# Splitting the first expert's weight chunks at other steps of the last head pair, in an attention and mixture-of-experts kernel

## The chip, the cores and the metric

The kernel runs on one core of one Trainium2 chip. A core has five engines that work side by side, each through its own list of instructions in order: TensorE (PE; its weight loads, PEld, overlap the matmuls), VectorE (DVE), ScalarE (ACT), GpSimd (POOL) and SyncE (SP), which here only issues DMA transfers. Engines wait for one another through semaphores. The metric is the time of one execution on the device in microseconds; lower is better. Times come as medians of several runs, and one further execution is recorded by the hardware profiler.

## What is computed

Attention over 8 batches and 8 heads, with queries averaged in pairs, and then a mixture of 8 experts on its output, each token going to the one expert with the highest logit:

```python
    q_pool = q.reshape(B, H, S // factor, factor, D).mean(axis=3)
    scores = scale * np.matmul(q_pool, k.transpose(0, 1, 3, 2))
    scores = scores - np.max(scores, axis=-1, keepdims=True)
    attn = np.exp(scores)
    attn = attn / (np.sum(attn, axis=-1, keepdims=True) + 1e-09)
    return np.matmul(attn, v).astype(np.float32)
...
    logits = x @ w_gate + modality_bias[modality_id]
    e_idx = np.argmax(logits, axis=1)
...
    for e in range(E):
        mask = e_idx == e
        h = np.maximum(x[mask] @ w1[e], 0.0)
        out[mask] = gate_w[mask, None] * (h @ w2[e])
```

Sizes: sequence 1152 (576 pooled queries), head width 64, 4608 tokens of 512 values, w1 of 512 x 1024 and w2 of 1024 x 512 for each expert. Inputs are f32; the kernel keeps f32 accuracy by splitting operands into a high and a low 16-bit part and multiplying three times.

## The kernel before

**Attention.** Two batches are taken together, so there are 32 pairs of heads. Each pair takes 18 steps of a loop (`for t in range(NSTEP * npairs)` in `attention`), 576 in all. A step emits work in a fixed order of letters: maximum pass of a later pair (`maxpass`: matmuls on PE, line 837, and reductions on DVE, line 838), score matmuls (lines 904 and 905) with their exponentials on ACT (line 906), and value products (`pv`, lines 963 to 965). A value product takes three matmuls for 128 queries: the high part of the exponentials `Pe` with the high and the low values, and the low part `Pl` with the values. `Pl` is made from `Pe` by a *lowering* (line 887 on ACT, 889 on DVE). Four pairs of buffers `Pe`/`Pl`, numbered 0 to 3, go round; one holds three of the nine key chunks of a head. After the last value product of a head, `evac` (lines 981 to 986) divides by the sums, and `split_x` (lines 923 and 933) splits the output into high and low parts.

Other work is hung into the steps. A table of numbers says at which step, counted from the pair's first, each piece is emitted; `at(t, p, fn)` puts it at the end of step `t`, `later(n, fn)` n steps on. Beside this there is a list of side jobs written as Python generators: `yield n` means "go on n steps later". For each of the four groups of 9 token tiles, `route` computes from the logits the gate values and the expert of each token; after group 2, `first_list` makes the token lists of the first six blocks of the expert stage (blocks 0 to 5) from the first three groups. Its steps follow one after another from where `route` ends.

**The last pair** (steps 558 to 575) has no maximum pass beside it. There the first expert is prepared, in four pieces per weight matrix: `load_first` loads chunk q of w1 into a tile of the attention that is no longer used (`rawq`, two of `rawk`, `rawv`), at the steps in `T_W0`; `split_first` splits it at the steps in `T_W1`: the high part on ACT (line 1584, 128 x 1024) and, at the end of the same step, the low part on DVE (line 1586). `gather_first` and `turn_first` gather and transpose the tokens of block 0 (`xfirst`, lines 1208 to 1222).

**Experts.** Blocks of 256 tokens, one expert each, follow on PE without a pause: `gemm1` multiplies by w1 (lines 1312 to 1314, 96 matmuls), `gemm2` by w2 (lines 1411 to 1413). The next chunks come through five raw buffers: `load_w` on SP's queue (line 1280 for w1, 1283 for w2), `split_w` on ACT and DVE (lines 1295 and 1296); a load waits until the chunk that used its buffer is split. The tokens of block j are gathered by POOL (line 1198), split into `xs` (lines 1262, 1263) and turned by four DMA transposes on SP's queue into `xpart` (line 1268), a high and a low part for each half of 128 tokens; `gemm1` of the block needs all four. The expert stage's raw buffers and gather buffers lie where the attention's tiles lay, so the first loads and gathers wait for the last readers of those tiles, the splits of line 1586 among them.

The order on PE, ACT, DVE and POOL is the order of emission within a stage; where the attention ends and the experts begin, and for the transfers on SP, the recording layer interleaves instructions by its own estimate of when they can start. So moving a piece can also change what stands around it elsewhere.

Of the kernel before, what the change touches and what calls it, by code (L numbers as in the profile page):

```python
# [118 lines left out]
NF = 4  # L119
T_W0 = (1, 3, 2, 3)  # L120
W1D = 0
T_W1 = (6, 4, 10, 11)
E1 = 1
E2 = 0
COPY = (lambda nc: nc.vector.tensor_copy, lambda nc: nc.scalar.copy, lambda nc: nc.gpsimd.tensor_copy)
# [38 lines left out]
class Router:  # L164
# [113 lines left out]
    def route(self, g, eng):  # L278

        nc, sm, rs = self.nc, self.sm, RS[g]  # L280
        while self.added[g] < H // 2:
            yield 1
        big = [sm.tile([P, 3, NT, E], F32, name=f"wide{i}") for i in range(2)]
        lg = big[0][:, 0]
        nc.vector.tensor_reduce(lg, self.lg[g].rearrange("p t (w e) -> p t e w", w=3), op=ALU.add, axis=AX.X)
        ts = slice(g * NT, (g + 1) * NT)
        bc = lambda a: a.unsqueeze(2).broadcast_to([P, NT, E])
        be = lambda a: a.unsqueeze(1).broadcast_to([P, NT, E])
        w, w2 = big[0][:, 1], big[0][:, 2]
        inv = sm.tile([P, NT], F32, name="inv")  # L290
        nc.gpsimd.tensor_scalar(inv, self.mid[:, ts], -1.0, 1.0, op0=ALU.mult, op1=ALU.add)
        nc.gpsimd.tensor_tensor(w, be(self.b0[:, 0]), bc(inv), op=ALU.mult)
        nc.gpsimd.tensor_tensor(w2, be(self.b0[:, 1]), bc(self.mid[:, ts]), op=ALU.mult)
        nc.gpsimd.tensor_tensor(w, w, w2, op=ALU.add)
        yield rs
        nc.gpsimd.tensor_tensor(lg, lg, w, op=ALU.add)
        yield rs + 1
        mx = sm.tile([P, NT], F32, name="mx")
        nc.vector.tensor_reduce(mx, lg, op=ALU.max, axis=AX.X)
        nc.vector.tensor_tensor(lg, lg, bc(mx), op=ALU.subtract)  # L300
        yield rs
        nc.scalar.activation(w, lg, AF.Exp)
        key = big[1][:, 0]
        nc.vector.scalar_tensor_tensor(key, lg, 0.0, be(self.ieE), op0=ALU.is_ge, op1=ALU.mult)
        kmin = sm.tile([P, NT], F32, name="kmin")
        nc.vector.tensor_reduce(kmin, key, op=ALU.min, axis=AX.X)
        yield rs
        oh = sm.tile([P, NT, E], BF16, name="oh16")
        nc.vector.tensor_tensor(oh, key, bc(kmin), op=ALU.is_equal)
        yield 1  # L310
        nc.gpsimd.tensor_scalar(self.exp[:, ts], kmin, float(E), None, op0=ALU.add)
        yield rs
        sx = sm.tile([P, NT], F32, name="sx")
        nc.vector.tensor_reduce(sx, w, op=ALU.add, axis=AX.X)
        gt = sm.tile([P, NT, 2], F32, name="gt")
        ts2 = sm.tile([P, 2], F32, name="ts2")
        nc.vector.tensor_reduce(ts2[:, 0:1], self.scales[g].bitcast(F32), op=ALU.max, axis=AX.X)
        yield 1
        nc.gpsimd.tensor_scalar(sx, sx, EPS, None, op0=ALU.add)
        nc.gpsimd.tensor_scalar(ts2[:, 0:1], ts2[:, 0:1], 1.0 / XSC, None, op0=ALU.mult)  # L320
        yield 1
        nc.vector.reciprocal(ts2[:, 1:2], ts2[:, 0:1])
        nc.vector.reciprocal(gt[:, :, 0], sx)
        nc.vector.tensor_scalar(gt[:, :, 0], gt[:, :, 0], ts2[:, 0:1], 1.0 / WSC ** 2, op0=ALU.mult, op1=ALU.mult)
        nc.gpsimd.tensor_copy(gt[:, :, 1], ts2[:, 1:2].broadcast_to([P, NT]))
        eng.dma_start(out=self.xs[g * NT * P:(g + 1) * NT * P, DM:XW].rearrange("(t p) d -> p t d", p=P), in_=gt)
        yield rs
        for _ in range(self.lr - 1):
            yield
        pr = self.pm(4)[:, 0:(NT + 1) * E].rearrange("p (t e) -> p t e", e=E)  # L330
        nc.tensor.matmul(pr[:, 0:NT], self.up, oh, start=True, stop=False, skip_group_check=True)
        for s in range(NT):
            nc.tensor.matmul(pr[:, s + 1:], self.on, oh[:, s:s + 1].broadcast_to([P, NT - s, E]), start=False, stop=s == NT - 1,
                             skip_group_check=True)
        yield 1
        pos = big[1][:, 2]
        nc.vector.tensor_tensor(pos, pr[:, 0:NT], be(self.base), op=ALU.add)
        nb = self.keep.tile([P, E], F32, name="base")
        nc.vector.tensor_tensor(nb, pr[:, NT], self.base, op=ALU.add)
        self.base = nb  # L340
        yield rs
        nc.gpsimd.tensor_tensor(pos, pos, oh, op=ALU.mult)
        yield rs
        nc.vector.tensor_reduce(self.pos[:, ts], pos, op=ALU.add, axis=AX.X)
# [241 lines left out]
def attention(tc, ctx, att, ident, npairs, xpool, on_two, on_split, on_scale, jobs, side, set_pm, started, ahead, hip):  # L586
# [419 lines left out]
    def later_end(n, fn):  # L1006
        at_end.setdefault(now[0] + n, []).append(fn)

    def at(t, p, fn, end=True):
        if 0 <= p < npairs:  # L1010
            (at_end if end else todo).setdefault(max(t, 0), []).append(fn)
# [120 lines left out]
    if ahead:  # L1132
# [10 lines left out]
        for i in range(NF):  # L1143
            at(last + T_W0[i], 0, lambda i=i: ahead[2](i, room[i]))
            at(last + T_W1[i], 0, lambda i=i: later_end(W1D, ahead[3](i)))
    running, wait = [], 0
# [496 lines left out]
```

## Time and profile before

| | us |
|---|---|
| median of 3 runs (lowest, highest) | 1127.96 (1127.93, 1128.63) |
| the profiled execution, its own time | 1128.69 |
| span of its records | 1126.9 |
| granted TensorE clock, mean | 0.997 of full |
| DVE / ACT / POOL busy in the span | 86% / 81% / 37% |

The profile page gives for each engine the busy time in the span, and the trace answers further questions: busy time by stretch, instructions in order of time, and for each idle stretch of an engine the instruction that ended it (in brackets: idle us, and after the arrow the engine, the tile and the line that was waited for). A row of the timeline has the start in us, the duration, the engine, the line of the kernel, the operation, and output <- inputs; "x3" means that three in a row are merged. Matmuls are pipelined: one of 65 columns takes 0.19 us from start to end, but the next starts 0.03 us after it. `SPq` and `POOL DMA` rows are the issues of transfers, not the transfers themselves.

### The profile page before, as it was taken

To read this page: it belongs to the slowest core of one execution; us is meant where nothing else is said; L and a number is where in the kernel's file an instruction comes from. 1 tells how busy PE (TensorE), PEld (TensorE's weight loads), DVE (VectorE), ACT (ScalarE), POOL (GpSimd) and SP (SyncE) were. 2 spreads that over 40 slices of the span, in tenths; PEclk is the share of its full clock that TensorE was granted. 3 is DMA by queue.
4 is the path that set the end of the run, shared out by engine and by line. 5 is a ranking of instruction groups with operands and counts; after the bars stand their busy time and mean duration, and the time that the engine had idled before them with its cause. 6 is when DMAs were issued, how large, how long until landed. Compare 5 with 4: busy or idle time off the path is not lost. (4 is left out here: it accounts for less than half of the span.)

```text
span 1126.9 us, 36809 instructions
## 1 busy us (share of the span) xinstructions
PE 1102.1 (98%) x15053; PEld 812.6 (72%) x15053; DVE 972.7 (86%) x1971; ACT 914.8 (81%) x1469; POOL 413.9 (37%) x408
## 2 busy tenths in 40 slices
PE   7999999999999999999999999999999999999997
PEld 3777777777777777777777777777667667667674
DVE  7999999999999999999999999877997756756754
ACT  5999999999999999999999998876656656655654
POOL 7853344355434444443445333115213122121111
PEclk9999999999999999999999999999999999999999
DMA  7667757758769678678687563599999999999993
GB/s 230 181 184 171 194 161 188 186 156 190 172 164 208 155 179 181 165 179 190 163 185 170 160 149 94 147 310 282 281 265 269 309 284 275 277 280 281 270 267 107
DMA packets 175522, 232.67 MB, mean 206 GB/s; under 512 B 92303, under 2 KB 126751, under 8 KB 175344
## 3 DMA queue, kind: packets, MB, share of 16 engines
q1 hardware_dynamic: 169254, 210.45, 71.8%
q0 software_dynamic: 6080, 19.78, 6.5%
q8 instruction: 120, 1.97, 0.8%
q14 instruction: 58, 0.48, 0.1%
q10 hardware_dynamic: 10, 0.00, 0.0%
HBM read 146.11 MB, written 18.99 MB: 147 GB/s over the span
## 5 line engine op out<-in xcount | busy, mean ns | idle before, releaser
L906 ACT ACTIVATE Pe<-psc 128x432 int32<-128x432 f32 x768 | 376.9, 526 | 41.0 <-PE psc L905 32.4
L838 DVE TENSOR_REDUCE mp<-pm 128x1 f32<-128x512 f32 x566 | 371.6, 684 | 17.1 <-PE pm L837 10.4
L963 PE MATMUL xp<-VH,Pe 128*128 128x65 f16 x2880 | 372.5, 193 | 0.0
L965 PE MATMUL xp<-VS,Pl 128*128 128x65 f16 x2880 | 371.9, 193 | 0.4 <-DVE Pl L889 0.4
L964 PE MATMUL xp<-vl,Pe 128*128 128x64 f16 x2880 | 370.6, 192 | 0.0
L964 PEld LDWEIGHTS <-Pe 128*128 128x128 f16 x2880 | 267.6, 98 | 87.6
L905 PE MATMUL psc<-B 65*128 65x432 f16 (+2 forms) x1152 | 304.7, 287 | 1.0 <-DMA B<-mr 1.0
L904 PE MATMUL psc<-B 128*128 128x432 f16 (+2 forms) x1152 | 304.0, 286 | 1.7 <-ACT Pe L906 1.5
L963 PEld LDWEIGHTS <-Pe 128*128 128x128 f16 x2880 | 272.0, 98 | 42.7 <-issue 5.2
L965 PEld LDWEIGHTS <-Pl 128*128 128x128 f16 x2880 | 266.5, 97 | 0.6 <-DVE Pl L889 0.6
L887 ACT ACTIVATE Pl<-Pe 128x1152 f16<-128x1152 uint16 (+1 forms) x190 | 219.2, 1154 | 6.0
L837 PE MATMUL pm<-hi,QB 128*128 128x512 f16 x566 | 213.8, 379 | 4.1 <-DVE mp L838 3.0
L1314 PE MATMUL ph<-xpart,w1l 128*128 128x256 f16 x544 | 148.3, 273 | 0.0
L1312 PE MATMUL ph<-xpart,w1h 128*128 128x256 f16 x544 | 148.3, 273 | 0.0
L1313 PE MATMUL ph<-xpart,w1h 128*128 128x256 f16 x544 | 148.3, 273 | 0.0
L784 POOL TENSOR_SCALAR VH<-rawv,sc 128x512 f16<-128x512 f32 (+1 forms) x60 | 103.6, 1736 | 76.2 <-PE pm L837 35.6
L905 PEld LDWEIGHTS <-B 65*128 65x128 f16 x1152 | 112.8, 98 | 25.3 <-issue 2.5
L904 PEld LDWEIGHTS <-B 128*128 128x128 f16 x1152 | 112.5, 98 | 7.9 <-issue 2.5
L1318 DVE SCALAR_TENSOR_TENSOR hl<-ph,hh 128x512 f16<-128x512 f32 x72 | 49.7, 690 | 73.3 <-ACT hh L1317 47.8
L1317 ACT ACTIVATE hh<-ph 128x512 f16<-128x512 f32 x72 | 43.0, 598 | 84.8 <-PE ph L1314 81.6
L1412 PE MATMUL po<-w2l,hh 128*128 128x512 f16 x288 | 109.2, 379 | 0.0
L1413 PE MATMUL po<-w2h,hl 128*128 128x512 f16 x288 | 109.2, 379 | 0.0
(274 smaller groups left out, 1877.6 us busy)
## 6 DMA issues: line engine op xcount, KB each, us to landing
w2r<-in_w_dram SPq DMA_DIRECT2D x76, 512.0 KB
w1r<-in_w_dram SPq DMA_DIRECT2D x72, 512.0 KB
rawv<-in_att_dram SPq DMA_DIRECT2D x32, 576.0 KB
B<-hi SPq DMA_DIRECT2D x128, 144.0 KB
rawq<-in_att_dram SPq DMA_DIRECT2D x31, 576.0 KB
rawk<-in_att_dram SPq DMA_DIRECT2D x31, 576.0 KB
B<-qh SPq DMA_DIRECT2D x128, 72.0 KB
B<-lo SPq DMA_DIRECT2D x64, 144.0 KB
```

Source lines behind the costliest of these rows:

```text
L837: nc.tensor.matmul(pm, QB[p % 2][:, u], s["hi"][:, t * 512:(t + 1) * 512], start=True, stop=True)
L838: nc.vector.tensor_reduce(mp[:, u, t:t + 1], pm, op=ALU.max, axis=AX.X)
L887: nc.scalar.activation(low, rest, AF.Copy, scale=LOW)
L904: nc.tensor.matmul(o, b1[:, ks], b1[:, qs], start=True, stop=False, skip_group_check=True)
L905: nc.tensor.matmul(o, b2[:, ks], b2[:, qs], start=False, stop=True, skip_group_check=True)
L906: nc.scalar.activation(Pe[:, D + x0:D + x1], pt, AF.Exp, scale=1.0 / 16)
L963: nc.tensor.matmul(out, Ph[:, qs], vh[:, c, j, 0:D + 1], start=c == 0 and g == 0, stop=False, skip_group_check=True)
L964: nc.tensor.matmul(out[:, 0:D], Ph[:, qs], vl[:, c, j], start=False, stop=False, skip_group_check=True)
L965: nc.tensor.matmul(out, Pl[:, qs], vs[:, c, j, 0:D + 1], start=False, stop=c == NKC - 1, skip_group_check=True)
L1312: nc.tensor.matmul(o, hi[:, c, fs], xh[:, :, c], start=c == 0, stop=False)
L1313: nc.tensor.matmul(o, hi[:, c, fs], xl[:, :, c], start=False, stop=False)
L1314: nc.tensor.matmul(o, lo[:, c, fs], xh[:, :, c], start=False, stop=c == 3)
```

## The change

```diff
-T_W1 = (6, 4, 10, 11)
+T_W1 = (9, 6, 14, 16)
...
         nc.vector.reciprocal(ts2[:, 1:2], ts2[:, 0:1])
         nc.vector.reciprocal(gt[:, :, 0], sx)
+        if g == 2:
+            yield 1
         nc.vector.tensor_scalar(gt[:, :, 0], gt[:, :, 0], ts2[:, 0:1], 1.0 / WSC ** 2, op0=ALU.mult, op1=ALU.mult)
```

Chunk 0 is split at step 9 instead of 6 of the last pair, chunk 1 at 6 instead of 4, chunk 2 at 14 instead of 10, chunk 3 at 16 instead of 11. In `route` of the third group the multiplication of the gates, with the copy and the store behind it, goes one step later (step 475 instead of 474), and with it every later piece of `route` and `first_list` up to step 554, which is now 555. What is left of `first_list` at step 557 is emitted there at once, before and after. No instruction is added or removed. The two new lines move the numbers of all later lines by 2 in the changed kernel.

**The end of the last pair, on DVE.** `Pl_120` and `Pl_122` are the low parts of buffers 2 and 3, which hold the last six key chunks, `w1l` the low part of a weight chunk, `x_17728` the output of `evac`. Before:

```order
L889 TENSOR_SCALAR Pl_120<-Pe_119 128x864
L981 TENSOR_SCALAR rs<-xp 128x5
L982 RECIPROCAL rr<-rs 128x5
L986 SCALAR_TENSOR_TENSOR x_17728<-xp,sc,rr 128x5x64
L889 TENSOR_SCALAR Pl_120<-Pe_119 128x864
L1222 TENSOR_TENSOR xfirst<-pm,xfirst 128x256 x2
L889 TENSOR_SCALAR Pl_122<-Pe_121 128x864 x2
```

With the change:

```order
L891 TENSOR_SCALAR Pl_120<-Pe_119 128x864
L983 TENSOR_SCALAR rs<-xp 128x5
L984 RECIPROCAL rr<-rs 128x5
L988 SCALAR_TENSOR_TENSOR x_17728<-xp,sc,rr 128x5x64
L1588 SCALAR_TENSOR_TENSOR w1l_18284<-rawk,w1h_18283 128x1024
L891 TENSOR_SCALAR Pl_120<-Pe_119 128x864
L1224 TENSOR_TENSOR xfirst<-pm,xfirst 128x256 x2
L891 TENSOR_SCALAR Pl_122<-Pe_121 128x864
L1588 SCALAR_TENSOR_TENSOR w1l_18340<-rawv,w1h_18339 128x1024
L891 TENSOR_SCALAR Pl_122<-Pe_121 128x864
```

Chunks 2 and 3 now stand between the last lowerings; before they stood ahead of the first row shown.

**The same place on PE.** The last value products (`xp`) and the first matmuls of the first expert (`ph`). Before, all value products come first:

```order
L965 MATMUL xp<-VS_126,Pl_122 128x65
L1312 LDWEIGHTS w1h_18052
L1312 MATMUL ph<-xfirst,w1h_18052 128x256
L1313 LDWEIGHTS w1h_18052
L1313 MATMUL ph<-xfirst,w1h_18052 128x256
```

With the change seven matmuls of the expert stand ahead of the last 25 of the value products; these are the rows where they end:

```order
L1316 MATMUL ph<-xfirst,w1l_18147 128x256
L1314 LDWEIGHTS w1h_18146
L1314 MATMUL ph<-xfirst,w1h_18146 128x256
L967 LDWEIGHTS Pl_122
L967 MATMUL xp<-VS_126,Pl_122 128x65
L965 LDWEIGHTS Pe_121
L965 MATMUL xp<-VH_125,Pe_121 128x65
```

The seven stand right ahead of a matmul that needs the second half of `Pl_122`.

**The start of the experts, on SP.** `xpart_18595` is the turned input of block 1: `xs_18597` and `xs_18598` are the high and low part of its first half, `xs_18602` and `xs_18603` of its second; `w1r_18516` is the fourth chunk of w1 for block 1, `w2r_18518`, `18524`, `18559` and `18610` its chunks of w2, `w1r_18625` the first of block 2. Before:

```order
L1268 DMA_TRANSPOSE xpart_18595<-xs_18597 128x4x128
L1268 DMA_TRANSPOSE xpart_18595<-xs_18602 128x4x128
L1268 DMA_TRANSPOSE xpart_18595<-xs_18598 128x4x128
L1268 DMA_TRANSPOSE xpart_18595<-xs_18603 128x4x128
L1280 ISA
L1280 DMA w1r_18516<-in_w1_dram 128x1024
```

With the change (the middle is left out: the loads `w2r_18518`, `w2r_18524`, `w2r_18559`):

```order
L1270 DMA_TRANSPOSE xpart_18595<-xs_18597 128x4x128
L1270 DMA_TRANSPOSE xpart_18595<-xs_18598 128x4x128
L1282 ISA
L1282 DMA w1r_18516<-in_w1_dram 128x1024
...
L1285 DMA w2r_18610<-in_w2_dram 128x1024
L1282 ISA
L1282 DMA w1r_18625<-in_w1_dram 128x1024
L1270 DMA_TRANSPOSE xpart_18595<-xs_18602 128x4x128
L1270 DMA_TRANSPOSE xpart_18595<-xs_18603 128x4x128
```

The transposes of the second half have moved behind six loads.

## The prediction

> **What bounds the kernel now.** First the page's table of engines, then busy time by stretch, to see which engine sets the end in the stages that the change touches.
>
> ```profile
> PE 1102.1 (98%) x15053; PEld 812.6 (72%) x15053; DVE 972.7 (86%) x1971; ACT 914.8 (81%) x1469; POOL 413.9 (37%) x408
> 600.00:700.00 100.00, 96.22 (x1650) 74.04 (x1647) 96.85 (x242) 92.83 (x158) 41.14 (x34) 1.00 0.61 141
> 712.00:736.00 24.00, 22.57 (x485) 19.40 (x482) 19.37 (x45) 19.92 (x38) 5.17 (x4) 1.00 0.65 207
> 736.00:900.00 164.00, 164.00 (x1212) 113.07 (x1209) 134.22 (x235) 104.35 (x137) 42.76 (x42) 1.00 1.00 284
> 900.00:1100.00 200.00, 200.00 (x1386) 135.45 (x1385) 129.12 (x152) 118.36 (x152) 36.76 (x37) 1.00 0.99 275
> ```
>
> The columns of a stretch are its length and the busy time of PE, PEld, DVE, ACT and POOL, then the granted clock and the DMA share. PE is busy 98% of the span at full clock, and from 736 to 1100 us without a gap. So nothing but PE's own gaps can be won, and a gap made in the expert stage is added to the end in full, because no later gap absorbs it. The gaps that the change can reach lie in the last pair of heads, 712 to 736 us (24.00 - 22.57 = 1.43 us idle), and around the third group's gates, near 610 us. The chain that ended last tells little here: its lines hold 1% of the span together.
>
> The gaps of the last pair, in PE's timeline (start, duration, idle before and its releaser in brackets):
>
> ```profile
> 720.41 0.19 PE L965 MATMUL xp<-VS,Pl 128*128 128x65 f16 x1
> 721.17 0.28 PE L904 MATMUL psc<-B 128*128 128x288 f16 x1 [0.57 <-ACT Pe L906]
> 728.70 0.19 PE L964 MATMUL xp<-vl,Pe 128*128 128x64 f16 x1
> 728.73 0.19 PE L965 MATMUL xp<-VS,Pl 128*128 128x65 f16 x1
> 729.34 0.34 PE L904 MATMUL psc<-B 128*128 128x432 f16 x1 [0.42 <-ACT Pe L906]
> 730.27 0.19 PE L964 MATMUL xp<-vl,Pe 128*128 128x64 f16 x1
> 730.89 0.20 PE L965 MATMUL xp<-VS,Pl 128*128 128x65 f16 x1 [0.43 <-DVE Pl L889]
> ```
>
> In flow these matmuls start 0.03 us apart (728.70 and 728.73), so the real losses are 0.76, 0.61 and 0.62 us less 0.03 each: **1.90 us**, more than the idle column says. Their causes stand on ACT and DVE:
>
> ```profile
> 719.64 1.06 ACT L1584 ACTIVATE w1h<-rawk 128x1024 f16<-128x1024 f32 x1 [0.77 <-DMA rawk<-in_w_dram]
> 724.82 0.77 ACT L923 ACTIVATE x<-x,sc 128x576 f16<-128x576 f32 x1
> 725.90 1.06 ACT L1584 ACTIVATE w1h<-rawk 128x1024 f16<-128x1024 f32 x1
> 727.26 1.07 ACT L1584 ACTIVATE w1h<-rawv 128x1024 f16<-128x1024 f32 x1
> 726.99 1.22 DVE L1586 SCALAR_TENSOR_TENSOR w1l<-rawk,w1h 128x1024 f16<-128x1024 f32 x1
> 728.36 1.23 DVE L1586 SCALAR_TENSOR_TENSOR w1l<-rawv,w1h 128x1024 f16<-128x1024 f32 x1
> 726.14 0.38 DVE L275 TENSOR_TENSOR lg<-pm,lg 128x216 f32<-128x216 f32 x1
> 729.50 0.81 DVE L933 SCALAR_TENSOR_TENSOR x<-x,sc,x 128x576 f16<-128x576 f32 x1
> 730.75 0.75 DVE L1222 TENSOR_TENSOR xfirst<-pm,xfirst 128x256 f16<-128x256 f32 x2
> 732.35 0.55 DVE L986 SCALAR_TENSOR_TENSOR x<-xp,sc,rr 128x320 f32<-128x320 f32 x1
> 734.00 1.12 DVE L889 TENSOR_SCALAR Pl<-Pe 128x864 f16<-128x864 uint16 x2
> ```
>
> Chunk 1's ACT half waited 0.77 us for its load with the exponentials queued behind it, hence the gap at 721. Chunks 2 and 3 stand one exponential apart on ACT, and their DVE halves back to back, hence the gaps at 729 and 731.
>
> **The change, part by part.** Nothing is added or removed in work: four ACT operations of 1.06 us and four DVE operations of 1.2 us move later, and one DVE operation of the gates moves a step.
>
> *Splits.* Chunk 1 at step 6 comes after its load has landed and alone: 0.73 us is won. Chunk 0 at step 9 stands on ACT right behind the operation of line 923. That one starts at 724.82 now and, with PE 0.73 earlier, near 724.0; chunk 0's ACT half ends near 725.7. From there DVE has no gap until the last lowering. In the order of the changed kernel it does: low part of chunk 0 (1.2), logits (0.3), two lowerings of Pe1 with line 933 between (0.6 + 0.75 + 0.55), xfirst (0.65), lowering (0.5), evacuation (0.85), low part of chunk 2 (1.2), lowering (0.5), xfirst (0.65), lowering (0.5), low part of chunk 3 (1.2), lowering (0.55). That is 10.0 us by the rows above (each less about 0.08, by which neighbours overlap; a lowering is half of the row at 734.00, the evacuation is line 986 with two small ones ahead); it ends near 735.6. Now the same last lowering ends at 734.00 + 1.12 = 735.12. PE runs 1.9 us ahead of today up to its last score products, less about 0.2 before Pe1's lowering, and so is done with them near 731.9 (733.60 now: the row at 733.41 below, and 0.19 until the next). Then it meets three new waits, by the same running sum: Pe2's second lowering, behind chunk 2, is there at 732.65 and wanted two value products later, at 732.05; Pe3's first at 733.8, wanted at 733.4; Pe3's second, behind chunk 3, at 735.6, wanted at 734.4. The last is partly covered, because seven matmuls of the first expert now stand in front of it (96 of them take 736.0 to 746.6 in the row below, so 7 take about 0.76 us). After the last lowering PE has 25 matmuls left, 25 x 0.03 = 0.75 us: the attention ends at 736.3 with 0.76 us of the expert done, worth 735.55.
>
> ```profile
> 733.41 0.35 PE L905 MATMUL psc<-B 65*128 65x432 f16 x1
> L1312 PE MATMUL ph<-xfirst,w1h x32: 272/273/276, 736.0 to 746.6; 128*128 128x256 f16 x32
> ```
>
> Now the first expert starts at 736.0, so the gain is **0.45 us** of the 1.90. Bounds: 1.90 won if DVE catches up, 0.8 lost if DVE ends 0.5 late and the seven matmuls cover nothing. I take 0.45.
>
> *What the splits free.* The raw tiles hold buffers that the expert's loads and gather need:
>
> ```profile
> 728.25 3.03 SPq L1283 DMA_DIRECT2D w2r<-in_w_dram  x4
> 729.85 1.28 POOL L1198 DMA_INDIRECT xg<-xs,giA  x1 [12.24 <-DVE w1l L1586]
> 743.39 5.51 SPq L1268 DMA_TRANSPOSE xpart<-xs  x4
> 749.16 0.37 SPq L1280 DMA_DIRECT2D w1r<-in_w_dram  x1
> 753.65 1.06 ACT L1295 ACTIVATE w1h<-w1r 128x1024 f16<-128x1024 f32 x1 [2.90 <-DMA w1r<-in_w_dram]
> 755.99 1.76 SPq L1280 DMA_DIRECT2D w1r<-in_w_dram  x2
> 757.80 0.27 PE L1312 MATMUL ph<-xpart,w1h 128*128 128x256 f16 x1
> ```
>
> The first load starts at 728.25, when chunk 2's low part ends (726.99 + 1.22), the gather when chunk 3's does (728.36 + 1.23). With chunk 2's end near 732.1 and chunk 3's near 735.0 both come 4 to 5 us later. What covers this: w2's first chunk is needed by line 1411 only after the 96 matmuls of w1, which end at about 747, and the gathered rows by the transposes at 743.39. These covers hold; if they were gone, up to 5 us would show.
>
> The cost that I do count is on SP's queue. All four transposes of block 1 now stand together at 743.39, 5.51 / 4 = 1.38 us each. In the changed kernel the second half's two stand behind six more loads. The last of the six waits until the fourth w1 chunk of block 1 is split on DVE. That chunk's load, held until 749.16 now, goes right after two transposes, near 746.2; its ACT half no longer waits 2.90 us but stands behind its neighbour, done at 751.75; its DVE half at 753.1 (1.2 each). So the sixth load goes at 753.2 and the two transposes at 753.5 and 754.8. When does such data arrive?
>
> ```profile
> DMA packets 504, 0.18 MB, mean 368 GB/s; under 512 B 489, under 2 KB 489, under 8 KB 504
> DMA packets 48, 0.20 MB, mean 393 GB/s; under 512 B 0, under 2 KB 0, under 8 KB 48
> 757.96 1.19 SPq L1268 DMA_TRANSPOSE xpart<-xs  x1
> DMA packets 314, 0.18 MB, mean 360 GB/s; under 512 B 286, under 2 KB 286, under 8 KB 314
> ```
>
> These are the DMA packets of 750.0 to 750.5, of 757.0 to 757.5 (loads alone: no small packets) and of 761.0 to 761.5. Small packets mark the transposes. Block 1's fourth, issued from 747.5 (743.39 + 5.51 - 1.38), was still moving at 750.0 to 750.5, 3.0 us after its start; block 2's first, issued at 757.96 among loads, at 761.0 to 761.5, 3.0 to 3.5. So the last transpose, from 754.8, is there at 757.8 to 758.3. PE wants it at 757.80 - 0.45 - 0.1 = 757.25. Stall: **0.5 to 1.1 us, I take 0.6**; bounds 0 (if the fourth chunk goes earlier) and 3 (if the loads that start 5 us later push the whole chain by 1.5 us, and the transposes wait among loads for 1 us more).
>
> The Trainium skill, "DMA: Bandwidth & Descriptors", section "Anatomy of one DMA — SWDGE (gpsimd) path", speaks against the change here: a transfer's semaphore fires only when the last byte is confirmed written, about 2.0 us of fixed cost. No row here shows that lag by itself; by it the stall would be near 2.5 us, and the sum, as an estimate, 1.9 us slower; that outcome is a rival below.
>
> *Gates.* DVE is full in this stage (96.85 of 100 us).
>
> ```profile
> 609.70 0.23 DVE L324 TENSOR_SCALAR gt<-gt,ts 128x9 f32<-128x9 f32 x1
> 609.84 0.68 DVE L838 TENSOR_REDUCE mp<-pm 128x1 f32<-128x512 f32 x1
> 610.58 0.38 PE L845 MATMUL pm<-hi,QB 128*128 128x128 f16 x4 [0.90 <-DVE mp L838]
> 611.97 0.38 PE L837 MATMUL pm<-hi,QB 128*128 128x512 f16 x1 [0.46 <-DVE mp L838]
> ```
>
> PE waits 0.90 us for the reduction at 609.84. One operation ahead of it (609.84 - 609.70 = 0.14 us) moves behind the next two: the reduction ends 0.14 earlier, **0.15 us** won. The small write of the gates now stands behind three moves on SP; only the gathers after the token list read it. Everything of this group up to the token list slides one step too: the same operations, between other reductions, on a DVE that stays full. Bounds for gates and slide together: 1.4 won (0.90 and the 0.46 behind it) and 0.7 lost. I take 0.15.
>
> **Sum**: -0.45 + 0.6 - 0.15 = 0.0 us, against the profiled execution's 1128.69 (span 1126.9 and 1.79 around it), which lies 0.73 above the median shown. On the median that is **1128.0 us**.
>
> **Rivals.**
> *All gaps close.* If the exponentials run ahead and DVE recovers, 1.90 + 0.15 go and the fourth chunk's early load lets the transposes land in time: 1128.0 - 2.05 = 1125.9; with the two gaps at 610 also gone (1.36 in place of 0.15), 1124.7. For it: each cause named above is really moved. Against it: DVE works 10.0 us without pause up to the last lowering.
> *Block 1 starved.* Slower: the second half of the tokens arrives 3 us late because the chain of six loads starts late; 3 - 0.6 = +2.4, 1130.4. It decides from the point where the fourth w1 chunk is split after 754.7 instead of 753.1. For it: DMA is full from 750 on, and block 2's transpose took over 3 us among loads. Against it: between 743 and 749 SP has been waiting, so the loads can catch up.
> *Late arrival.* The transposes count as arrived about 2 us after their last packet: stall 2.5 in place of 0.6, 1129.9. For it: the load issued at 749.16 was used on ACT only at 753.65, 4.5 us later, although 0.5 MB take 1.3 us at the 393 GB/s of the packets above. Against it: four more loads shared the engines with that one. The skill's fixed cost, quoted above, is this case.
> *Nothing moves.* PE only swaps three gaps for others and the transposes land in time: 1128.0 - 0.6 = 1127.4.
>
> **How the numbers follow.** Chances: the forecast 0.45 (its own range 1126.8 to 1129.4), all gaps close 0.20, block 1 starved 0.16, late arrival 0.10, nothing moves 0.09. A difference below about 0.2%, 2.26 us, cannot be told from no change here. Of the second case about half, 0.11, passes it on the fast side; of the third 0.10 passes it on the slow side; the rest, 0.79, is the same. The range leaves out the ends of these two cases: 1125.6 to 1130.3.
>
> **What would show it.** Right: the brackets at 721 and 729 gone; new waits of line 965's weights on `Pl` near 732 to 735; seven matmuls of the first expert among the last value products; the first `w2r` load near 732; PE's first matmul of block 1 with an idle bracket of about half a microsecond released by the transposes. Wrong: a stall of 2 us or more at that matmul (the starved case), none at all there together with no waits near 733 (the fast case), or any new wait of PE for `w2h`, which I held covered.

## The result, and the profile after

The changed kernel takes **1142.6 us** (median of 4 runs, 1140.76 to 1143.62) against 1127.95 (4 runs beside it, 1127.76 to 1128.63): 1.0127 times the time before, interval 1.0111 to 1.0142. It is slower, by 14 us, and the prediction of 1128.0 was wrong. The profiled execution took 1140.76 us with a span of 1139.0, 12.1 us more than the span before.

The page's table of engines and three stretches of the changed kernel (columns as in the prediction):

```profile
PE 1107.8 (97%) x15053; PEld 814.5 (72%) x15053; DVE 974.6 (86%) x1971; ACT 915.6 (80%) x1469; POOL 414.3 (36%) x408
712.00:736.00 24.00, 22.77 (x470) 19.34 (x467) 19.46 (x46) 19.48 (x38) 2.56 (x2) 1.00 0.45 145
736.00:900.00 164.00, 155.49 (x1139) 105.35 (x1137) 126.04 (x227) 96.29 (x126) 40.57 (x42) 0.98 0.99 274
900.00:1100.00 200.00, 200.00 (x1392) 135.97 (x1390) 132.21 (x154) 121.77 (x156) 39.51 (x38) 1.00 0.99 276
```

The 97% of the first row hides it. The last pair is as good as before, and from 900 us on PE is full again; between 736 and 900 PE now stands still for 164 - 155.49 = 8.5 us, and its granted clock is 0.98 there. Before it had neither. PE's waits from 715 to 800 us (total us, times, longest):

```profile
PE ph L1314 <- DMA xpart<-xs: 4.6, 1, 4.6
PE pmr L252 <- ACT xt L253: 3.6, 1, 3.6
PE xp L967 <- DVE Pl L891: 1.2, 4, 0.6
```

The third row is the predicted one. The other two are new, and the timeline shows how they hang together (all engines of the changed kernel, in order of time; lines are 2 higher than before):

```profile
733.45 4.78 SPq L1285 DMA_DIRECT2D w2r<-in_w_dram  x4
736.53 1.07 POOL L1200 DMA_INDIRECT xg<-xs,giA  x1 [17.92 <-DVE w1l L1588]
751.69 1.06 ACT L1297 ACTIVATE w1h<-w1r 128x1024 f16<-128x1024 f32 x1 [4.77 <-DMA w1r<-in_w_dram]
752.77 1.23 DVE L1298 SCALAR_TENSOR_TENSOR w1l<-w1r,w1h 128x1024 f16<-128x1024 f32 x1 [5.07 <-ACT w1h L1297]
753.60 0.57 ACT L253 CAST xt<-pmr 128x512 f16<-128x512 f32 x1
754.03 0.34 SPq L1282 DMA_DIRECT2D w1r<-in_w_dram  x1
754.21 0.38 PE L252 MATMUL pmr<-id,x 128*128 128x128 f16 x4 [3.64 <-ACT xt L253]
761.66 1.06 ACT L1297 ACTIVATE w1h<-w1r 128x1024 f16<-128x1024 f32 x1 [3.03 <-DMA w1r<-in_w_dram]
762.75 1.23 DVE L1298 SCALAR_TENSOR_TENSOR w1l<-w1r,w1h 128x1024 f16<-128x1024 f32 x1 [3.01 <-ACT w1h L1297]
764.00 0.33 SPq L1282 DMA_DIRECT2D w1r<-in_w_dram  x1
764.38 2.50 SPq L1270 DMA_TRANSPOSE xpart<-xs  x2
768.91 0.37 PE L1314 MATMUL ph<-xpart,w1h 128*128 128x256 f16 x1 [4.58 <-DMA xpart<-xs]
```

Read it from the top. Block 0's gather goes at 715.75 here and at 714.81 before; counted from it, the loads start 4.3 us and the gather 5.7 us later than before (728.25, 729.85). Block 1's first w1 chunk is then late, and ACT waits 4.77 us for it; before, this split ran at 743.81 without a wait (6.9 us earlier, counted in the same way). ACT works in order, so the copy `xt` of the side job stands behind it, and PE waits 3.64 us: the first stall. The chunk's low part ends at 752.77 + 1.23 = 754.00, and in that moment, at 754.03, the load of the fourth w1 chunk goes (749.16 before). Its split ends at 762.75 + 1.23 = 763.98, the sixth load goes at 764.00, the held transposes at 764.38, and PE waits 4.58 us for them: the second stall. Block 1 starts at 768.91 instead of 757.80.

And why the chunk is late at all: two stretches of the kernel before, then the same two of the changed one (the last two numbers are the DMA share and the GB/s moved):

```profile
728.00:738.00 10.00, 9.14 (x182) 8.07 (x180) 8.64 (x20) 6.69 (x15) 3.00 (x3) 1.00 0.87 288
736.00:748.00 12.00, 12.00 (x114) 10.33 (x111) 10.24 (x17) 8.90 (x14) 3.36 (x3) 1.00 1.08 257
728.00:738.00 10.00, 8.78 (x180) 7.40 (x177) 8.87 (x20) 6.11 (x13) 1.17 (x2) 1.00 0.23 70
736.00:748.00 12.00, 11.82 (x131) 10.42 (x129) 8.00 (x15) 5.89 (x9) 4.14 (x5) 1.00 0.84 266
```

From 728 to 738 the DMA moves 10 x 70 = 0.7 MB instead of 2.9 MB. In the 12 us from 736 it moves 3.2 MB, and 3.1 MB before: almost nothing is made up. The load of this chunk itself goes at 738.43, 22.7 us after block 0's gather, against 731.47 and 16.7 us before: 6.0 us later. Before, the chunk was taken 12.3 us after its load went and without a wait, so some of that time was cover; now ACT waits for it and takes it 13.3 us after its load went.

### The profile page after: what moved, and what is told of

It reads as the page before. It is cut to its first block, busy times and chain, and to the rows that moved or that the text cites. A ratio compares the mean times of both kernels' runs of the same rounds, so it can differ in the third digit from the quotient of the medians.

```text
span 1139.0 us, 36809 instructions
## 1 busy us (share of the span) xinstructions
PE 1107.8 (97%) x15053; PEld 814.5 (72%) x15053; DVE 974.6 (86%) x1971; ACT 915.6 (80%) x1469; POOL 414.3 (36%) x408
## 5 line engine op out<-in xcount | busy, mean ns | idle before, releaser
L1413 PE MATMUL po<-w2h,hh 128*128 128x512 f16 x288 | 109.9, 382 | 0.0
```

## The experiments

All ratios are to the kernel before, run beside each on the same chip, with 95% intervals. Where nothing else is said, the order on all engines but SP is that of the kernel each run is derived from.

| run | ratio | interval |
|---|---|---|
| the change | 1.0127 | 1.0111 to 1.0142 |
| e1 steps only, no extra step of the gates | 1.0118 | 1.0095 to 1.0141 |
| e2 chunks 2 and 3 in tiles of their own | 1.0004 | 0.9991 to 1.0016 |
| e3 SP order alone | 1.0026 | 1.0012 to 1.0041 |
| e4 the change with the old SP order | 1.0074 | 1.0051 to 1.0097 |
| e5 own tile for chunk 2 alone | 1.0118 | 1.0103 to 1.0134 |
| e6 own tile for chunk 3 alone | 1.0009 | 0.9998 to 1.0020 |
| e7 steps 9, 6, 10, 11 | 1.0010 | 1.0001 to 1.0020 |
| e8 steps 9, 6, 12, 13 | 1.0008 | 0.9999 to 1.0017 |
| e9 gather late alone | 1.0016 | 1.0006 to 1.0025 |
| e10 loads late alone | 1.0074 | 1.0051 to 1.0096 |
| e11 steps 9, 6, 13, 15 | 1.0039 | 1.0025 to 1.0053 |
| e12 late, no transposes of block 1 | 1.0041 | 1.0027 to 1.0056 |
| e13 late, no gather of block 2 | 1.0080 | 1.0057 to 1.0104 |
| e14 late, one half of the transposes held | 1.0107 | 1.0087 to 1.0127 |
| e15 late, all four transposes held | 1.0094 | 1.0073 to 1.0115 |
| e16 late, w2 splits first | 1.0058 | 1.0038 to 1.0078 |
| e17 before, w2 splits first | 1.0000 | 0.9989 to 1.0011 |

**e1, the gates.** The kernel before with one line changed:

```diff
-T_W1 = (6, 4, 10, 11)
+T_W1 = (9, 6, 14, 16)
```

> The steps (9, 6, 14, 16) without the gates' extra step. Theory L (the late splits of chunks 2 and 3 hold the tiles that the expert's first loads and gathers need, DMA cannot catch up): all of the loss stays, 1.012 to 1.014 times the time before (about 1142 us), with the waits for xt near 752 and for xpart near 765. Rival G (the gates' step makes the loss): back to 1128.

All of the loss stays, with both stalls (4.2 and 7.7 us in its profile). The gates' step does nothing that these runs can tell.

**e2, the raw tiles.** The changed kernel; the attention's raw tiles for chunks 2 and 3 are replaced by two tiles above all others in the on-chip buffer:

```diff
             a, *r = [pa.tile([P, S], F32, name="raw" + x) for x in "qqkkv"]
+            r[2:4] = [spare.tile([P, 4 * TB], F32, name=f"spare{i}") for i in range(2)]
```

> The changed kernel, but the raw data of chunks 2 and 3 lie in two tiles of their own, above all others, so that no expert load or gather waits for their splits; the splits stand at steps 14 and 16 as in the change. The order of the transposes on SP is then that of before. Theory L: the loss goes whole, 1126.5 to 1128.5 us, the first w2r load near 727 or earlier. Rival K (the late splits cost on DVE, ACT and PE themselves, by the order of work in the last pair): 1140 or more stays. Rival S (the order on SP alone makes the loss): also about 1128, so this run does not tell L from S.

SP's first loads, and all of PE's waits from 715 to 800 us, in this run:

```profile
724.48 7.20 SPq L1287 DMA_DIRECT2D w2r<-in_w_dram  x4
PE xp L968 <- DVE Pl L892: 1.2, 4, 0.6
```

The splits are as late as in the change, PE has the same four waits for `Pl`, and the loss is gone. So it isn't the work in the last pair that costs, but what the splits hold. Rival K falls. SP's order is that of before here too, so e3 and e4 take the two apart.

**e3, the order on SP.** The kernel before; the second half's transposes are tied behind the sixth load (`issue_after` sets an order on one queue and adds no wait):

```diff
-                nc.sync.dma_start_transpose(out=o[:, h], in_=x)
+                with tc.issue_after(B[2]["l", 0].ins) if j == h == 1 else ExitStack():
+                    nc.sync.dma_start_transpose(out=o[:, h], in_=x)
```

> The kernel before, every engine's order unchanged, but on SP the transposes of block 1's second half stand behind six more loads, as in the changed kernel; loads and gathers are as early as before. My prediction's own term: +0.6 us (0 to 3), 1127.6 to 1131. Rival S (the order on SP is the whole cause): +5 us or more, with a PE wait for xpart of over 4 us.

```profile
755.64 2.51 SPq L1269 DMA_TRANSPOSE xpart<-xs  x2
760.53 0.27 PE L1313 MATMUL ph<-xpart,w1h 128*128 128x256 f16 x1 [1.20 <-DMA xpart<-xs]
761.02 0.27 PE L1314 MATMUL ph<-xpart,w1h 128*128 128x256 f16 x1 [0.22 <-DMA xpart<-xs]
```

With early loads the moved transposes cost 1.4 us of PE's time. The span is 2.7 us longer, but 1.4 of that is there at the first load already (729.62, 728.25 before). Rival S falls as the whole cause.

**e4, the change with the old order on SP.** The loads from the eighth on are written behind the transposes, so that these stand together again (4 rows of SP differ from the changed kernel, nothing else):

```diff
-        fetch(4)
+        fetch(2)
...
+                if i == 0 and s == 2:
+                    fetch(6)
```

> The changed kernel, every other engine's order unchanged, but on SP all four transposes of block 1 stand together ahead of the load of its fourth w1 chunk, as before. Theory L: the late loads remain, so the wait for xt near 752 stays (3 to 5 us with its clock loss) and only the second stall shrinks: 1131 to 1137 us. Rival S: back to 1128 (plus 0 to 2).

+0.74%, some 8 us at the upper edge of what theory L gave, with the wait for `xt` at 3.6 us as in the change. So the order on SP, worth 1.4 us with early loads, is worth 5 to 6 us (1.0127, or 1.0118 in e1, against 1.0074) when the chain ahead of it is late.

**e5 and e6, which chunk.** As e2, with one own tile, for chunk 2 (e5) or chunk 3 (e6, `r[3]`):

```diff
+            r[2] = spare.tile([P, 4 * TB], F32, name="spare")
```

> The changed kernel with a tile of its own for the raw data of chunk 2 alone: the first w2r load goes at about 724, but the second and, behind it in SP's queue, all others still wait for chunk 3's split near 735, and so does the gather. Everything else stands in the order of the changed kernel. Theory L: one load of 512 KB is out of the way, the rest is as late as before: 1136 to 1142 us. If chunk 2 were what holds the loads: back to 1128 to 1130.

> The changed kernel with a tile of its own for the raw data of chunk 3 alone: the gather goes early (about 724) and the loads all wait for chunk 2's split, near 732, instead of 728. Theory L with the gather and chunk 3 as the hold that counts: 1128 to 1131 us. If every late microsecond of the loads counted in proportion (4 of 5 to 7 us): 1136 or more. The order on SP is that of the kernel before.

Chunk 3, split at step 16, holds nearly everything: the second load and behind it, in SP's queue, all others, and the gather. With its tile apart the loss is gone, though all loads still wait for chunk 2's split. SP's order differs between the two runs, so each is read against its own: e5, with the order of the change, is 1.0118 against 1.0127; e6, with the order of before, 1.0009 against e4's 1.0074. SP in e6:

```profile
733.10 2.20 SPq L1287 DMA_DIRECT2D w2r<-in_w_dram  x4
```

Block 0's gather goes at 715.29 in this run, so the loads are 3.6 to 4.4 us later than before, and it costs nothing that can be told; block 1's gather runs ahead of them here (718.46). The loss is not in proportion to the delay.

**e7, e8 and e11, how late is too late.** The kernel before with other steps; SP's order is that of before in all three:

```diff
-T_W1 = (6, 4, 10, 11)
+T_W1 = (9, 6, 10, 11)    e8: (9, 6, 12, 13)    e11: (9, 6, 13, 15)
```

> The kernel before, with chunks 0 and 1 alone moved (steps 9 and 6), chunks 2 and 3 at their old steps 10 and 11. Theory L: nothing is late, the gap at 721 is gone: 0 to 1 us faster than before, 1127 to 1128.5. Rival (moving any chunk later costs): above 1131.

> Steps (9, 6, 12, 13): chunks 2 and 3 two steps later than before, so first loads near 730.5 and gather near 732.5, 2 to 3 us late instead of 5 to 7; SP's order is that of before. Theory L with a cover of a few microseconds: 0 to +3 us, 1127 to 1131. Proportional loss: +5 to +6.

> Chunks 2 and 3 one step earlier than in the change (13 and 15), SP's order that of before: loads from about 731.5 and 734, the gather near 735. The same order on SP with steps 14 and 16 cost +0.7%; steps 12 and 13 cost nothing. If the cover ends between: +1 to +6 us, 1129 to 1134. If the loss comes as a step at once: either below +1 or above +7.

Two steps later cost nothing that can be told, steps 13 and 15 cost 4.4 us, 14 and 16 (e4, same order on SP) 8.3. The loss comes abruptly: chunk 3's low part ends 19.2 us after block 0's gather in e8 and 19.3 in e11, as DVE is full, and only chunk 2's split, and so the first load, comes 1.7 us later in e11. The load of block 1's first w1 chunk goes at 21.0 and 21.1 us after block 0's gather. Yet ACT takes the chunk 8.9 us after that without a wait in e8, and 13.7 us after it in e11 (first e8, then e11):

```profile
734.35 7.03 SPq L1280 DMA_DIRECT2D w1r<-in_w_dram  x3
743.20 1.05 ACT L1295 ACTIVATE w1h<-w1r 128x1024 f16<-128x1024 f32 x1
734.65 7.35 SPq L1280 DMA_DIRECT2D w1r<-in_w_dram  x3
748.33 1.06 ACT L1295 ACTIVATE w1h<-w1r 128x1024 f16<-128x1024 f32 x1 [5.16 <-DMA w1r<-in_w_dram]
```

So it isn't only the start of the loads that counts. In the profiles the chunk is taken 8.2 to 8.9 us after its load goes in e6, e8, e10 and e12 (in e6 and e8 without a wait), but 12.3 to 13.7 us after it in the change and in the eight other runs in which ACT waits over 3 us for it. What makes the load take the longer time is not shown.

e7 is a miss: it was to be 0 to 1 us faster and is 0.10% slower. It leaves 0.27 us of the gap at 721, but PE's waits in the last pair are 2.4 us in sum, 1.4 before. From block 0's gather to the start of the first expert's last matmul it takes 746.95 - 713.83 = 33.1 us, and 746.77 - 714.81 = 32.0 before. So it doesn't test what the closed gap is worth.

**e9 and e10, gather or loads.** The kernel of e2, in which nothing waits, with one added wait on chunk 3's split: for block 1's first gather (e9), or for the second load (e10). The order on every engine is that of e2.

```diff
+        tc.add_manual_dep(this.ins, first["s", 3].ins.name, sync, reason="as late as chunk 3")
```

> The kernel with the tiles of its own (its time was that of before), and block 1's gather alone made to wait for chunk 3's split, as late as in the changed kernel (near 736); the loads go early. Every engine's order is that of the kernel with own tiles. If bytes that start late are what counts (two gathers of 0.26 MB each are 0.5 of the 4 MB): 0 to +3 us, 1127 to 1131. If the gathered rows were the ones that hold everything: +6 us or more.

> The same kernel, but the second w2r load, and in SP's queue all loads behind it, made to wait for chunk 3's split (near 735); the gather goes early. If the late bytes of the loads count: +2 to +8 us with the wait for xt behind w1h near 750, 1130 to 1136. If only the gathered rows hold everything: 0 to +2.

The gather alone costs 0.16%, the loads alone 0.74%. In e10 one load goes at 723.80 and the rest behind chunk 3's split, which ends at 735.94. Counted from block 0's gather, the second load then goes 3.7 us later than in e6, and the run costs 7 us more. The wait for `xt` near 750 that was expected is not in e10's profile; that recorded one of the two faster of its five runs (1133.57), and the other three took 1136.48 to 1137.66.

**e12 to e15, why 5 us become 14.** From 748 to 760 us the DMA moves 188 GB/s in the changed kernel and 346 before. Theory T was that the transposes, running among late loads, slow them.

In e12, and likewise for block 2's gather in e13 (`j == 2`):

```diff
+                if j == 1:
+                    nc.gpsimd.memset(o[:, h], 0.0)
+                else:
                     nc.sync.dma_start_transpose(out=o[:, h], in_=x)
```

> The changed kernel without block 1's four transposes: its turned input is filled with zeros by GpSimd instead, so block 1's result is left out; every other engine's order is unchanged. Theory T (transposes that run among loads slow the loads): the DMA rate from 748 to 760 stays near 300 GB/s instead of 188, the wait for xt shrinks to below 1.5 us, and there is no second stall: 1127 to 1131. Rival B (the late bytes alone: the queue is simply too long): the first w1 chunk of block 1 still lands near 751, the wait for xt stays near 3.6 us, 1132 or more.

> The changed kernel without block 2's gather (its rows are set to zero by GpSimd, so block 2's result is left out), which the trace of the changed kernel shows at 745.7 and 748.0, among the late loads. Theory T: little changes, 1138 to 1143. Rival B or a rival by which the gathers slow the loads: 0.53 MB less at the critical time, 1135 or less.

In e14 for one half (`h == 0`), from the changed kernel, and in e15 for both, from e4:

```diff
+                if j == 1:
+                    tc.add_manual_dep(this.ins, b["l", 2].ins.name, sync, reason="behind the loads")
```

> The changed kernel with all its work and order, but the first two transposes of block 1 wait until the three w1 loads ahead of them on SP have landed. Theory T: the loads land near 747 to 748 instead of 751.7, the wait for xt shrinks by 2 us or more, and with it the chain behind: 1130 to 1138. Rival B: the loads land no earlier and the transposes come later still: 1142 or more.

> The late splits with the four transposes of block 1 together on SP (the run that measured +0.74%), and these four also wait until the three w1 loads ahead of them have landed; the loads behind them stay behind. In the run before, only the half that stood later was held, so it did not test this. Theory T: the first w1 chunk lands 3 to 4 us earlier, the wait for xt falls from 3.6 to below 1.5 us, and the loss from 8.3 us to 2 to 6: 1130 to 1134. Rival B: the loads land no earlier, and the transposes start 3 us or more later than before: 1138 or more.

e12's profile spoke for T: a wait for `xt` of 0.4 us only, 330 GB/s. But it recorded the fastest of five runs (1130.33); the others took 1133.42 to 1134.52, in rival B's range, and a run without block 1's transposes can't have the second stall. Without block 2's gather some 5 of the 14 us go (e13; 1138.65, at the lower edge of what theory T gave). e14 tested nothing: the recording layer put the half that was free ahead of the held one, so that only the halves changed places. e15 held all four until the three w1 loads had landed; SP's wait for that, and ACT's for the first of them:

```profile
SPq L1270 <- DMA w1r<-in_w_dram: 9.6, 1, 9.6
749.26 1.06 ACT L1302 ACTIVATE w1h<-w1r 128x1024 f16<-128x1024 f32 x1 [4.54 <-DMA w1r<-in_w_dram]
```

With no transpose in the way ACT waits 4.54 us, as long as ever (4.77), and the time, 1137.99, is no better than e4's, where theory T gave 1130 to 1134. So the first stall doesn't need the transposes, and theory T falls as its cause. That the bytes ahead of the chunk make it late, as rival B has it, is argued and not shown. Up to this load e12 and e15 issue the same loads at the same times after block 0's gather, and neither has a transpose of block 1 behind them before ACT takes the chunk; it does so 12.5 us after the load in e15's profile, but 8.9 us after it in e12's (first e15, whose row of ACT stands above, then e12):

```profile
736.75 6.04 SPq L1287 DMA_DIRECT2D w1r<-in_w_dram  x3
738.57 11.54 SPq L1285 DMA_DIRECT2D w1r<-in_w_dram  x4
747.43 1.06 ACT L1300 ACTIVATE w1h<-w1r 128x1024 f16<-128x1024 f32 x1 [1.43 <-DMA w1r<-in_w_dram]
```

**e16 and e17, ACT's order.** On ACT and DVE the splits of block 0's third and fourth w2 chunk go ahead of the split of the late chunk, and that one behind `xt` and `hh` of its step; as in e4, the loads behind the fourth w1 chunk's are written behind the transposes. e17 does the same to the kernel before.

```diff
-                    split_w(0, 4 + s)
+                    for q in ((4,), (5, 6), (7,), ())[s]:
+                        split_w(0, q)
...
-                    split_w(*pieces[k])
+                    for n in ((), (), (8,), (9, 10))[s] if i == 0 and s < 4 else (k,):
+                        split_w(*pieces[n])
```

> The changed kernel with its late splits, raw tiles and gather as they are; on ACT and DVE the splits of block 0's third and fourth w2 chunk, whose data are there, stand ahead of the split of block 1's first w1 chunk, whose load is late, and that chunk's split stands behind the copy xt and hh of its step. On SP the four transposes of block 1 stand together, behind the load of the fourth w1 chunk (the comparison is the run with the old order of SP, 1137.4). Theory A (the delay grows because ACT works in order: the late chunk holds xt, and the splits that free raw buffers, so the next loads are issued late): the wait for xt goes below 1 us, the fourth w1 load is issued near 746 instead of 754 to 758, the loss falls to 0 to +4 us, 1127 to 1131. Rival B (the late bytes alone): +6 or more, 1133 and up.

> The kernel before with the same reordering on ACT, DVE and SP. Nothing waits there for the late chunk, so theory A expects no change: 1126 to 1129, within 0.2% of before. If it is faster by over 0.2%, the in-order hold costs in the kernel before too.

In e16, ACT, SP and PE:

```profile
746.10 0.58 ACT L253 CAST xt<-pmr 128x512 f16<-128x512 f32 x1
750.50 1.06 ACT L1298 ACTIVATE w1h<-w1r 128x1024 f16<-128x1024 f32 x1 [3.32 <-DMA w1r<-in_w_dram]
744.79 11.62 SPq L1270 DMA_TRANSPOSE xpart<-xs  x4
760.33 0.40 PE L1315 MATMUL ph<-xpart,w1h 128*128 128x256 f16 x1 [2.62 <-DMA xpart<-xs]
```

The first stall is gone: `xt` no longer stands behind the late chunk, and the fourth w1 load goes ahead of the transposes, before 744.79. So ACT's order did pass the delay on to PE and to the next loads. But the loss only falls to 0.58% (1133.95, in the range given for rival B), not to the 0 to 4 us that theory A gave, and against e4's 0.74% the intervals overlap. A second stall stays: from the first transpose to the end of the last are 11.62 us now (5.51 before). Nearly all of that is in the four issues themselves, 1.27 + 2 x 2.21 + 5.73 = 11.4 us; a single one took up to 5.7 us, as the row of this line shows (shortest, median, longest in ns; e16, then the kernel before, there with two of block 2):

```profile
L1270 SPq DMA_TRANSPOSE xpart<-xs x4: 1267/2210/5733, 744.8 to 753.4; - x4
L1268 SPq DMA_TRANSPOSE xpart<-xs x6: 1189/1242/1549, 743.4 to 759.8; - x6
```

Theory A is right on the first stall; the rest it does not explain. The control e17 is the same as before, so the reordering is worth nothing where loads are early.

No version beat the kernel before: of the runs none is below 1.0000.

## Why the prediction was wrong

**The step that failed** is the cover: "What covers this: w2's first chunk is needed by line 1411 only after the 96 matmuls of w1 ... and the gathered rows by the transposes at 743.39. These covers hold". It looked at the first load and the rows, each by itself. The first did hold: PE has no wait for `w2h`. But behind the first load stand six more and the gather, and the sum let all of them be late at no price; only the bound of 3 and the rival "block 1 starved" let them push, by 1.5 us. The reason I gave was that "between 743 and 749 SP has been waiting, so the loads can catch up". That misread a row of the prediction: from 743.39 to 748.90 SP issues the four transposes. It waits before that, 9.1 us in two waits between 731 and 743, for buffers to be split. And what SP does is not what the DMA does: in the kernel before, the DMA moves 257 GB/s from 736 to 748. Some catching up is possible, as the same stretch shows in e6 and e8, which lose nothing that can be told:

```profile
736.00:748.00 12.00, 11.82 (x129) 10.29 (x128) 10.04 (x17) 9.32 (x14) 3.36 (x3) 1.00 1.07 317
736.00:748.00 12.00, 12.00 (x109) 10.09 (x107) 10.05 (x17) 8.81 (x14) 3.36 (x3) 1.00 1.09 311
```

That is 0.6 to 0.7 MB more than the 3.1 MB of before. The changed kernel, with 2.2 MB less by 738, moves 266 GB/s there, 0.1 MB more, and block 1's first w1 chunk is split 6.9 us later. Why it makes up so little is not shown.

**What the cover cost.** Own tiles remove all of the loss (e2), chunk 3's alone too (e6). Late loads by themselves cost 0.74% (e10).

**How it grew.** The first stall was not in the prediction at all, the second only in a rival: ACT, in order, passes one late chunk on to a copy that PE waits for (3.64 us; e16 takes it away), the chunk's buffer holds the next load, and that load the transposes (4.58 us). The two stalls and 0.2 us make 8.4 of the 12.1 us; the lower clock behind each stall, below, makes 3.2 more, and 0.9 us are there already at block 0's gather. That is 0.4 us too much in sum.

**The term for SP's order** (+0.6, bounds 0 to 3) was right in kind: 1.4 us in e3, where loads are early. There the last transpose, issued at 755.64 + 1.25 = 756.9, was used at 761.02, 4.1 us later, not 3.0 to 3.5. The fixed cost that the prediction cited from the Trainium skill, "DMA: Bandwidth & Descriptors", section "Anatomy of one DMA — SWDGE (gpsimd) path", would have made the stall 2.5; the measured 1.4 lies between the two. These transposes go from SP, not from GpSimd.

**The rival "block 1 starved"** had the mechanism of the second stall and the right point of decision: a fourth chunk split after 754.7; it was split at 763.98. Its price of +2.4 and its chance of 0.16 rested on loads pushed by 1.5 us, that is on the same cover.

**The other terms.** The gaps at 721 and 729 went, and four waits for `Pl` of 1.2 us in all came, as said. The gain of 0.45 us did not come: from block 0's gather to the start of the first expert's last matmul it takes 747.65 - 715.75 = 31.9 us, and 32.0 before. The running sum for DVE starts at 725.55 where the text before it has 725.7, a slip of 0.15 us that changes nothing. The gates' 0.15 us can't be told from nothing (e1 against the change).

**What stays open:** why ACT gets block 1's first w1 chunk 8 to 9 us after its load in some runs and 12 to 14 us after it in others; why a single transpose takes up to 5.7 us to issue among late loads (in e15, where the three w1 loads ahead had landed, all four take 5.14 us), and so the larger part of e16's remaining 0.58%; and how much of the loss the transposes' own traffic makes, since e12's runs spread over 4 us.

## What to carry to other kernels

A late consumer holds a buffer, and whoever waits for the buffer may be a whole queue: count everything behind the first waiting transfer, and set the bytes against what the stretch in which they are to be made up is seen to move, not against what the issuing engine does there. Loss can come abruptly: two steps were free, four to five cost 8 us, and 14 with another order on one queue. Where an in-order engine serves both late data and a copy that the critical engine needs, look whether the copy can go first; here that took a stall of 3.6 us away (e16), though the gain in time over e4 is not clear of the noise.

## What the runs showed of the hardware

PE's clock can drop after a stall. Stretches behind stalls (granted clock third from the end): two of the changed kernel, then one each of e16, e11, e13, e6 and e2; the two last lie behind waits near 661 us:

```profile
754.93:758.34 3.41, 3.41 (x10) 1.23 (x9) 3.41 (x5) 3.41 (x6) 0.00 (x0) 0.50 1.36 110
768.58:771.99 3.41, 2.97 (x22) 2.02 (x22) 1.98 (x2) 2.82 (x4) 0.49 (x1) 0.50 1.06 268
760.34:763.75 3.41, 3.41 (x32) 2.41 (x33) 0.70 (x1) 1.64 (x3) 0.00 (x0) 0.50 0.96 384
750.85:754.26 3.41, 3.41 (x22) 1.82 (x22) 3.41 (x4) 3.41 (x6) 0.00 (x0) 1.00 0.98 67
753.20:756.61 3.41, 3.41 (x22) 1.80 (x22) 3.41 (x4) 3.41 (x6) 0.00 (x0) 1.00 0.74 207
661.60:665.01 3.41, 3.40 (x35) 2.58 (x36) 3.29 (x8) 1.69 (x2) 0.67 (x1) 0.50 0.04 8
663.75:667.16 3.41, 3.41 (x58) 2.61 (x59) 3.34 (x8) 2.48 (x4) 0.67 (x1) 1.00 0.03 8
```

In these seven, behind stalls of 3.64, 4.58, 2.62, 2.28, 3.13, 2.00 and 2.00 us, the clock is at 0.50 for 3.41 us or not lowered at all. The length of the stall alone doesn't decide: 2.00 us in e6 were followed by the half clock, 2.00 us in e2 and 3.13 us in e13 were not; every stall of 3.57 us or more, nine in six runs, was. Busy time times what is missing of the clock gives, for the two stretches of the changed kernel, 3.41 x 0.5 + 2.97 x 0.5 = 3.2 us, so each such stretch cost 1.5 to 1.7 us beyond its stall. The Trainium skill, "TensorE: Matmul & The Clock Gate", section "Why this matters for your kernels", has the rule: no idle gaps of over about 3 us, or the clock falls back to half. The runs agree on the half clock, but not on the bound: here 2.00 us were enough in e6, and 3.13 us were not in e13.

A DMA share near 1 says little of the rate: 346 GB/s before and 188 in the changed kernel from 748 to 760, at shares of 1.00 and 1.14.
